# The order of the two late parts, and the last layer of expert 1 by columns, in a recurrent-attention-then-MoE kernel

## The chip, the cores and the metric

The kernel runs on one core of a Trainium2 chip. The metric is the device time of one execution in microseconds, as the median of several runs. One further execution is profiled; its trace has every instruction of TensorE (PE, with its weight loads as PEld), VectorE (DVE), ScalarE (ACT), GpSimd (POOL) and the queue of SyncE (SP).

## The reference, cut to what matters

```python
for t in range(S):                                   # B=4, H=8, S=768, D=48
    state = alpha[:, :, t, :, None] * state + k_t outer v_t
    y[:, :, t] = einsum('bhd,bhde->bhe', q[:, :, t], state)
x = y.transpose(0, 2, 1, 3).reshape(3072, 384)
# mixture of experts: 4 groups of 4 experts, F = 1024
g = argmax(x @ w_group);  e = argmax(x @ w_expert[g])
out[token] = g_w * e_w * (relu(x @ w1[g, e]) @ w2[g, e])
```

Every token goes to one of 16 experts, with the product of two softmax weights as its factor. Both layers of an expert have 384 x 1024 weights. Everything is float32.

## The kernel before, in words

**First part.** The recurrence runs in 24 chunks of 128 steps. The instructions of this part are put in order by a planner (class `Plan`, emitted at L1151): each operation has an engine, an assumed duration, the operations it comes after, and sometimes a `lead`; `level` is the longest way from an operation to the end, and of the operations that an engine could start within a patience of 0.4 us the one of the highest level goes next. PE's order and SP's order are written out by hand (`row="pe"`, `row="sp"`). The 24 chunks end in groups of tokens whose expert is chosen on DVE; each chunk's 128 rows are then scattered to the experts' slots in DRAM by an indirect DMA issued from POOL (`scatter` at L744, planned at L761). These 24 scatters are a row of their own, in which `rest` is the planned pause after one before the next may start: `REST` = 0.7 for chunks before `AHEAD_T` = 18 and 0.1 after that. `EARLY_T` is 12. A pause is no instruction: only the resulting order of the instructions reaches the chip. After the last scatter the rows of the fullest expert are fetched and turned into columns (`xt_ahead`).

**Second part.** `jobs` is a list of 18: jobs 0 and 1 are the early parts of experts 0 and 1 (96 tokens each, from the first 12 chunks), jobs 2 to 15 the other 14 experts (224 - 8 - 3r tokens, 8 less for the last two; job 15 has 169), job 16 the late part of expert 0 (120 tokens) and job 17 that of expert 1 (96 tokens). The loop at L1378 runs over them in order. For each, `hidden` makes the first layer with tokens as the moving columns (L281), 8 blocks of 128 features in 4 pairs, each pair ended by a ReLU copy on ACT (L297). For jobs 1 to 15 `result` makes the second layer the same way, "by columns": w2 is the stationary side and the tokens are the moving columns; for at most `FEW` = 124 tokens each product is made in two halves of 64 weight columns (`product`, L279). ACT copies the result to `yT` (L308). In the next job's `hidden`, `deliver_quarters` turns it back to rows on DVE (L1187), multiplies by the factors (L1190) and yields one POOL scatter of 128 quarter rows (96 floats) for each block of 32 tokens (L1194). `destined` works out the row numbers on DVE (L1229, L1237); its tile `dst_q` has two buffers, so the one of job j is written when the scatters of job j-2 are done.

Jobs 16 and 17 carry the mark `by_token`. Their second layers are kept until both first layers are done, and then made by `last_rows`, one after the other: here the hidden tokens are the stationary side and 256 and 128 columns of w2 move (L1359); DVE and ACT multiply by the factor in `marks` while copying out (L1366, L1364), and one POOL scatter of whole rows (384 floats) ends each (L1368). The scatters of job 15 are spread behind the ReLU copies of jobs 16 and 17 (`scattered` with `behind`, which puts a one-column POOL copy, L1204, ahead of a scatter).

A loop at L1411 over tokens beyond the fixed capacities follows; it turns as many times as there are such blocks.

Of the kernel before, what the change touches and what calls it, by code (L numbers as in the profile page):

```python
# [110 lines left out]
def gla_then_hierarchical_moe(  # L111
# [54 lines left out]
    FIXED, EARLY, CAPS = 2, (96, 96), (216, 192)  # L166
    LOW = 144
    FEW = 124
    EARLY_T, AHEAD_T = (B - 2) * NC, (B - 1) * NC
# [146 lines left out]
    jobs = [fixed_job(e, 0, n) for e, n in enumerate(EARLY)]  # L316
    jobs[0]["hT"] = cp.tile([P, FC, EARLY[0]], F32, name="early_hT")
    jobs += [dict(r=r, c0=0, n=cap(r), nb=-(-cap(r) // 32)) for r in range(NS)]
    jobs += [dict(e=e, c0=n, n=CAPS[e] - n, nb=-(-(CAPS[e] - n) // 32)) for e, n in enumerate(EARLY)]
    for job in jobs[-FIXED:]:  # L320
        job["by_token"] = True
    ahead = jobs[FIXED]
    ahead["rows"] = cp.tile([P, ahead["nb"], QW], F32, name="rows_ahead")
    ahead["xt"] = cp.tile([P, DC, 32 * ahead["nb"]], F32, name="xt_ahead")
# [56 lines left out]
    with ExitStack() as gla:  # L381
# [323 lines left out]
        def add_send(g, b, c0, c1, counted, weighed, after_scatter):  # L705
# [51 lines left out]
            for c in range(C):  # L757
                if C < 3:
                    plan.add(f"touch{t0 + c}", POOL, 0.1, partial(touch, t0 + c),
                             after=[f"kept_r{t0 + c}"])  # L760
                plan.add(f"scatter{t0 + c}", POOL, 1.1, partial(scatter, c),  # L761
                         after=[f"touch{t0 + c}" if C < 3 else None, placed, weighed, "rowids", f"fill{FILLS - 1}", *after_scatter],
                         row="scatter", lands=2.0, lead=LEAD if t0 + c < EARLY_T else 0.0,
                         rest=REST if t0 + c < AHEAD_T else 0.1)
                if t0 + c in BETWEEN:
                    us, fn = BETWEEN[t0 + c]
                    plan.add(f"between{t0 + c}", POOL, us, fn, row="scatter")
# [390 lines left out]
    def hidden(w1, xt, n, between={}, behind={}):  # L1158
        hT = mp.tile([P, FC, CAP], F32, name="hT")
        for f0 in range(0, FC, 2):  # L1160
            for fn in between.get(f0, ()):
                fn()
            relu(hidden_pair(w1, xt, n, f0), n, hT, f0)
            for fn in behind.get(f0, ()):
                fn(behind=hT[:, f0])
        return hT
# [172 lines left out]
    def deliver_last(k=NB):  # L1339
        waiting.extend(deliver_quarters(*pending.popleft()))  # L1340
        scattered(waiting, k)
# [28 lines left out]
            in_=yo[0:n], in_offset=None, bounds_check=N - 1, oob_is_err=False)  # L1370

    cnt, rank, order, _ = numbered
    kept = []
    fetch_rows(jobs[FIXED + 1])
    pending.append((jobs[0], results[0], destined(jobs[0])))
    results.reverse()
# [1 line left out]
    for j, job in enumerate(jobs):  # L1378
        if j == 0:
            continue  # L1380
        if j + 3 < len(jobs):
            fetch_rows(jobs[j + 3])
        width = job["n"]
        w1, w2 = weights.pop(j)
        whole = "by_token" not in job
        dst = destined(job) if whole else None
        if whole:
            hT = hidden(w1, xt, width, {2: [deliver_last] if pending else []})
        elif pending:
            one = partial(scattered, waiting, 1)  # L1390
            hT = hidden(w1, xt, width, {2: [partial(deliver_last, 1)]}, {4: [one]})
        else:
            hT = hidden(w1, xt, width, {}, {0: [one], 4: [one], 6: [partial(scattered, waiting, NB)]})
        if j + 2 < len(jobs):
            load_weights(j + 2, expert(jobs[j + 2]))
        if not whole:
            kept.append((job, w2, hT))
        if job is jobs[-1]:
            break
        xt = ahead["xt"] if jobs[j + 1] is ahead else columns(jobs[j + 1])  # L1400
        if j == 4:
            excess, ceiling = ceilings()
            first, whose, n_more = left_over()
        if whole:
            pending.append((job, result(w2, hT, width), dst))
    for a in kept:
        last_rows(*a)

    n_left = nc.values_load(n_more[0:1, 0:1], min_val=0, max_val=NX,
                            skip_runtime_bounds_check_because="a count of at most NX")  # L1410
# [92 lines left out]
```

## Time and profile before

| | |
|---|---|
| median of 3 runs | 383.19 us (381.73 to 383.92) |
| the profiled execution | 381.04 us |
| its span, first to last instruction | 379.2 us |
| PE busy | 369.1 us |
| POOL busy | 200.8 us |
| mean granted clock of TensorE | 0.997 |

The profiled execution's own time is 1.84 us above its span, and 2.15 us below the median of the three runs. The trace is read by groups of instructions, by the chain of work that ended last (followed back from the last instruction, at each step to what released it), by timelines of one engine, and by windows that give each engine's busy time in a stretch. In a timeline a line is start, duration, engine, source line, operation, output from input with their shapes; a line with xN merges N instructions that follow one another, of which it names the first's shape; in brackets is the idle time of the engine before it and what ended it.

### The profile page before, as it was taken

Reading aid. Unit: us, or ns where it says so; the run is one execution under the profiler, and the core shown is the slowest. Engines: PE = TensorE matmul, PEld = TensorE weight load, DVE = VectorE, ACT = ScalarE, POOL = GpSimd, SP = SyncE. Lnnn points to the kernel's source line nnn. Section 1 sums busy time; section 2 is a strip of 40 time slices with the busy share of each in tenths; the row PEclk is TensorE's granted clock in tenths of the full one; section 3 lists DMA queues with packets and bytes.
Section 4 is the critical chain, followed back from the end, with each engine's and each line's share of the span. In section 5 each row is a group of like instructions: output and inputs, shape, how many; then the busy total and the mean of one; then the engine's idle time right before and its main releaser. Section 6 shows DMA issues by size and latency. Waiting matters only on the chain.

```text
span 379.2 us, 10153 instructions
## 1 busy us (share of the span) xinstructions
PE 369.1 (97%) x4120; PEld 350.5 (92%) x4120; DVE 157.5 (42%) x346; ACT 119.5 (32%) x315; POOL 200.8 (53%) x241
## 2 busy tenths in 40 slices
PE   7899999999999999999999999999999999999994
PEld 5788888888879999999999999999999999999983
DVE  7799899998866420238202022020220211201200
ACT  2666757866653220211112121121211212111210
POOL 6898779999876042616254261634525326236251
PEclk9999999999999999999999999999999999999998
DMA  7999997879873599999976475866769667755001
GB/s 276 397 401 399 409 402 265 267 252 338 329 240 149 165 295 346 344 352 361 339 247 217 183 244 227 285 225 209 235 238 300 218 200 247 284 199 192 8 22 37
DMA packets 30787, 98.08 MB, mean 259 GB/s; under 512 B 18040, under 2 KB 19764, under 8 KB 26131
## 3 DMA queue, kind: packets, MB, share of 16 engines
q1 hardware_dynamic: 25955, 87.87, 66.6%
q0 software_dynamic: 4784, 9.55, 7.3%
q8 instruction: 33, 0.54, 0.6%
q14 instruction: 15, 0.12, 0.1%
HBM read 85.76 MB, written 12.07 MB: 258 GB/s over the span
## 4 chain that ended last, share of the span: by engine, by line
PE 93%; DVE 2%; issue 1%; DMA 1%; ACT 1%; POOL 0%; POOLq 0%; DVEq 0%
PE bank L281 63%; PE zs L503 6%; PE zo L569 6%; PE bank L592 5%; PE zo L578 3%; PE zo L532 3%; PE bank L545 3%; PE zs L281 2%; PE bank L1359 2%; DVE kd L469 1%; DVE cq L480 1%; DMA in<-in_rows_dram 1%; PE bank L781 1%; ACT yt L584 0%; POOL in L489 0%
## 5 line engine op out<-in xcount | busy, mean ns | idle before, releaser
L1194 POOL DMA_INDIRECT out_dram<-yq,dst_q x98 | 95.4, 974 | 146.0 <-DVE yq L1190 109.6
L281 PE MATMUL bank<-hT,w 128*64 128x96 f32 (+14 forms) x768 | 117.5, 318 | 0.0
L281 PEld LDWEIGHTS bank<-hT,w 128*128 128x128 f32 (+1 forms) x768 | 115.5, 183 | 0.0
L281 PE MATMUL bank<-xt_e,w 128*64 128x120 f32 (+14 forms) x816 | 113.5, 311 | 0.0
L281 PEld LDWEIGHTS bank<-xt_e,w 128*128 128x128 f32 (+1 forms) x816 | 111.6, 178 | 0.2 <-issue 0.2
L1237 DVE SCALAR_TENSOR_TENSOR dst_q<-xq,past_q 128x7 int32<-128x7 int32 (+1 forms) x13 | 2.2, 166 | 150.5 <-DMA out_dram<-yq,dst_q 150.5
L297 ACT ACTIVATE hT<-bank 128x192 f32<-128x192 f32 (+15 forms) x68 | 32.0, 471 | 97.7 <-PE bank L281 74.8
L308 ACT COPY yT<-bank 128x192 f32<-128x192 f32 (+28 forms) x30 | 11.9, 396 | 98.5 <-PE bank L281 98.5
L746 POOL DMA_INDIRECT slots_d<-xr,place x24 | 24.1, 1006 | 6.7 <-issue 3.6
L592 PE MATMUL bank<-wr,yt 112*64 112x116 f32 x384 | 25.7, 267 | 0.3 <-ACT yt L584 0.3
L592 PEld LDWEIGHTS bank<-wr,yt 112*64 112x64 f32 x384 | 20.6, 137 | 1.0 <-ACT yt L584 0.5
L1187 DVE STREAM_TRANSPOSE yq<-yT 128x672 f32<-128x672 f32 (+2 forms) x16 | 12.6, 789 | 18.3 <-ACT yT L308 18.3
L485 POOL TENSOR_TENSOR in<-in,kd 112x512 f32<-112x512 f32 (+1 forms) x15 | 16.7, 1118 | 5.9 <-DVE kd L469 5.9
L517 ACT COPY sm<-zs 128x512 f32<-128x512 f32 x27 | 15.8, 588 | 12.2 <-PE zs L503 11.1
L558 ACT ACTIVATE state<-sums,kd 112x48 f32<-112x48 f32 x64 | 17.9, 334 | 3.0 <-DVE sums L554 2.8
L469 DVE TENSOR_TENSOR_SCAN kd<-in,starts 112x516 f32<-112x516 f32 (+1 forms) x15 | 17.0, 1140 | 4.1 <-DMA in<-in_rows_dram 3.1
L489 POOL TENSOR_TENSOR in<-in,cq 112x512 f32<-112x512 f32 (+1 forms) x16 | 16.9, 1058 | 3.4 <-DVE cq L480 3.3
L503 PE MATMUL zs<-in 48*64 48x128 f32 (+1 forms) x352 | 16.2, 274 | 2.3 <-POOL in L489 2.2
L520 POOL TENSOR_SCALAR_AFFINE_SELECT sm<-sm 128x512 f32<-128x512 f32 x27 | 17.0, 641 | 1.6 <-ACT sm L517 1.5
L480 DVE TENSOR_TENSOR_SCAN cq<-in,starts 112x516 f32<-112x516 f32 (+1 forms) x16 | 17.3, 1090 | 1.1
L503 PEld LDWEIGHTS zs<-in 48*64 48x64 f32 (+1 forms) x352 | 13.5, 148 | 4.0 <-POOL in L489 3.2
L584 ACT COPY yt<-zo 112x512 f32<-112x512 f32 x24 | 14.1, 586 | 8.5 <-PE zo L578 6.6
(161 smaller groups left out, 406.0 us busy)
## 6 DMA issues: line engine op xcount, KB each, us to landing
w<-in_w_dram SPq DMA_DIRECT2D x36, 1536.0 KB
in<-in_rows_dram SPq DMA_DIRECT2D x11, 962.5 KB
w<-in_rows_dram SPq DMA_DIRECT2D x10, 962.5 KB
xq<-slots_d SPq DMA_DIRECT2D x28, 85.8 KB
slots_d<-blank SPq DMA_DIRECT2D x2, 980.0 KB
xq<-slots_d SPq DMA_DIRECT2D x24, 73.5 KB
out_dram<-yq,dst_q POOLq DMA_INDIRECT x98
in<-in_rows_dram SPq DMA_DIRECT2D x4, 256.0 KB
```

The source lines that it names most:

```text
L281: nc.tensor.matmul(z[s], lhsT=w[:, s], rhs=x, start=first, stop=last, skip_group_check=True)
L297: nc.scalar.activation(out=hT[:, f0:f0 + 2, 0:n], in_=z[:, 0:2 * n].rearrange("p (f t) -> p f t", f=2), func=AF.Relu)
L469: nc.vector.tensor_tensor_scan(out=flat(c.kd[:, p0:p1])[:, ::-1], data0=c.t[0:R, A1 * p1:A1 * p0:-1], data1=one_col.to_broadcast([R, A1 * ...
L480: nc.vector.tensor_tensor_scan(out=flat(c.cq[:, p0:p1]), data0=c.t[0:R, A1 * p0:A1 * p1], data1=starts[0:R, A1 * p0:A1 * p1], initial=1.0, ...
L489: nc.gpsimd.tensor_tensor(out=c.q[:, p0:p1], in0=c.q[:, p0:p1], in1=c.cq[:, p0:p1, 1:A1], op=ALU.mult)
L503: nc.tensor.matmul(c.zs[i][s, p, :], lhsT=c.k[r, p, s], rhs=c.q[r, p, :], start=True, stop=True)
L520: nc.gpsimd.affine_select(out=c.sm[:, i], in_=c.sm[:, i], pattern=[[0, HP], [1, P]], compare_op=ALU.is_ge, fill=0.0, base=0, channel_multi ...
L558: nc.scalar.activation(out=c.st[:, p, 0:D], in_=chunks[c.n - 1].sums[:, p], func=AF.Copy, scale=c.kd[:, p, 0:1])
L569: nc.tensor.matmul(of(c.zo, p)[o], lhsT=c.v[:, h * D:h * D + o.stop - o.start], rhs=c.sm[:, i, p, :], start=(p < 2), stop=(c.bc == 0), ski ...
L592: nc.tensor.matmul(z[s, p * W:(p + 1) * W], lhsT=c.yt[:, p, s], rhs=wr[:, p, :], start=True, stop=True)
L746: sent = nc.gpsimd.indirect_dma_start(out=slots_by[t], out_offset=bass.IndirectOffsetOnAxis(ap=m["place"][:, c:c + 1], axis=0), in_=xr[:, ...
L1194: nc.gpsimd.indirect_dma_start(out=out_by.popleft().rearrange("n (j w) -> (n j) w", j=4), out_offset=bass.IndirectOffsetOnAxis(ap=dst[:, b ...
```

## The change

The two late parts change places: job 16 becomes expert 1's (96 tokens), job 17 expert 0's (120 tokens). Only job 17 keeps `by_token`. Job 16's second layer is now made by `result`, by columns, after the first layers of both jobs; its rows are then turned and scattered by `deliver_last` (three scatters of quarter rows), and `last_rows` of job 17 follows. Job 16 gets `destined` in place of the row numbers in `last_rows`, and no `marks`. The scatters of job 15 keep their places in the loop. In the planner, the pause after the scatters of chunks 12 to 17 becomes 1.0 in place of 0.7, and after those of chunks 18 and 19 1.0 in place of 0.1.

```diff
-    jobs += [dict(e=e, c0=n, n=CAPS[e] - n, nb=-(-(CAPS[e] - n) // 32)) for e, n in enumerate(EARLY)]
-    for job in jobs[-FIXED:]:
-        job["by_token"] = True
+    jobs += [dict(e=e, c0=EARLY[e], n=CAPS[e] - EARLY[e], nb=-(-(CAPS[e] - EARLY[e]) // 32))
+             for e in (1, 0)]
+    jobs[-1]["by_token"] = True
...
-                         rest=REST if t0 + c < AHEAD_T else 0.1)
+                         rest=(REST if t0 + c < EARLY_T else 1.0) if t0 + c < AHEAD_T + 2 else 0.1)
...
-        if whole:
+        if job in jobs[-2:]:
+            one = partial(scattered, waiting, 1)
+            hT = hidden(w1, xt, width, *(({}, {0: [one], 4: [one], 6: [partial(scattered, waiting, NB)]})
+                                         if job is jobs[-1] else
+                                         ({2: [partial(deliver_last, 1)]}, {4: [one]})))
+        else:
             hT = hidden(w1, xt, width, {2: [deliver_last] if pending else []})
-        elif pending:
-            one = partial(scattered, waiting, 1)
-            hT = hidden(w1, xt, width, {2: [partial(deliver_last, 1)]}, {4: [one]})
-        else:
-            hT = hidden(w1, xt, width, {}, {0: [one], 4: [one], 6: [partial(scattered, waiting, NB)]})
...
-        if not whole:
-            kept.append((job, w2, hT))
...
-        if whole:
+        if job is jobs[-2]:
+            held_back = (w2, hT, width), dst
+        else:
             pending.append((job, result(w2, hT, width), dst))
-    for a in kept:
-        last_rows(*a)
+    products, dst = held_back
+    pending.append((jobs[-2], result(*products), dst))
+    deliver_last()
+    last_rows(job, w2, hT)
```

## Rows read from the trace of the kernel before

**Rows 1.** The page, busy time of each engine (share of the span, instructions)
```profile
PE 369.1 (97%) x4120; PEld 350.5 (92%) x4120; DVE 157.5 (42%) x346; ACT 119.5 (32%) x315; POOL 200.8 (53%) x241
```

**Rows 2.** The chain that ended last, in order of time (start us, us, what)
```profile
123.67 239.53 PE bank L281 x1728
363.20 7.13 PE bank L1359 x41
...
374.93 0.53 POOL out_dram L1368
```

**Rows 3.** Timeline of all engines, the last 40 us (start us, us, engine)
```profile
340.50 0.17 DVE L1237 SCALAR_TENSOR_TENSOR dst_q<-xq,past_q 128x6 int32<-128x6 int32 x1 [11.29 <-DMA out_dram<-yq,dst_q]
...
349.44 0.97 POOL L1194 DMA_INDIRECT out_dram<-yq,dst_q  x1 [0.30 <-issue]
...
354.10 9.10 PE L281 MATMUL bank<-xt_e,w 128*64 128x120 f32 x192
...
354.59 0.78 DVE L1187 STREAM_TRANSPOSE yq<-yT 128x576 f32<-128x576 f32 x1 [11.70 <-ACT yT L308]
...
356.08 0.47 DVE L1211 STREAM_TRANSPOSE xt_e<-xq 128x288 f32<-128x288 f32 x1
...
363.13 10.66 PE L1359 MATMUL bank<-w,hT 128*120 128x256 f32 x64
...
366.09 0.97 POOL L1194 DMA_INDIRECT out_dram<-yq,dst_q  x1 [0.31 <-issue]
...
368.62 0.37 ACT L1364 ACTIVATE yo<-bank,marks 120x128 f32<-120x128 f32 x1 [4.91 <-PE bank L1359]
369.30 1.02 POOL L1368 DMA_INDIRECT out_dram<-yo,dst_m  x1 [2.23 <-ACT yo L1364]
...
373.87 0.36 ACT L1364 ACTIVATE yo<-bank,marks 96x128 f32<-96x128 f32 x1 [4.88 <-PE bank L1359]
374.52 0.94 POOL L1368 DMA_INDIRECT out_dram<-yo,dst_m  x1 [4.19 <-ACT yo L1364]
```

**Rows 4.** Timeline of PE, job 1's last layer and what follows it
```profile
127.68 4.13 PE L281 MATMUL bank<-hT,w 128*64 128x96 f32 x96
131.74 9.03 PE L281 MATMUL bank<-xt_ahead,w 128*128 128x216 f32 x48
```

**Rows 5.** Timeline of ACT, the last copy of job 1's result
```profile
131.85 0.24 ACT L308 COPY yT<-bank 128x96 f32<-128x96 f32 x1 [0.29 <-PE bank L281]
```

**Rows 6.** Timeline of DVE, the ahead columns and job 0's turn
```profile
130.29 0.88 DVE L810 STREAM_TRANSPOSE xt_ahead<-rows_ahead 128x672 f32<-128x672 f32 x1 [5.08 <-DMA rows_ahead<-slots_d]
...
131.72 0.47 DVE L1187 STREAM_TRANSPOSE yq<-yT 128x288 f32<-128x288 f32 x1
132.23 0.46 DVE L1190 TENSOR_TENSOR yq<-yq,rows 128x288 f32<-128x288 f32 x1
```

**Rows 7.** Windows of 0.25 us, last two DMAs (core us, busy, PEclk, DMA, GB/s)
```profile
370.75:371.00 0.25, 0.25 (x2) 0.16 (x1) 0.00 (x0) 0.00 (x0) 0.00 (x0) 1.00 0.81 166
...
371.50:371.75 0.25, 0.25 (x3) 0.20 (x2) 0.00 (x0) 0.00 (x0) 0.00 (x0) 1.00 0.39 148
...
376.00:376.25 0.25, 0.00 (x0) 0.00 (x0) 0.00 (x0) 0.00 (x0) 0.00 (x0) 1.00 1.10 295
...
376.50:376.75 0.25, 0.00 (x0) 0.00 (x0) 0.00 (x0) 0.00 (x0) 0.00 (x0) 0.88 0.38 84
```

**Rows 8.** Windows of 1 us, after the scatters of job 14
```profile
351.00:352.00 1.00, 1.00 (x10) 1.00 (x9) 0.00 (x0) 0.00 (x0) 0.00 (x0) 1.00 0.04 7
```

**Rows 9.** Timeline of POOL, the scatter of the last chunk
```profile
121.88 0.98 POOL L746 DMA_INDIRECT slots_d<-xr,place  x1 [0.98 <-DVE cnt L348]
```

**Rows 10.** Windows by stage of the first part
```profile
60.00:85.00 25.00, 25.00 (x575) 21.88 (x572) 23.46 (x43) 17.23 (x51) 23.81 (x25) 1.00 0.80 272
85.00:113.60 28.60, 27.81 (x593) 23.46 (x591) 22.27 (x64) 17.42 (x52) 23.94 (x27) 1.00 0.86 304
113.60:123.70 10.10, 9.72 (x207) 9.10 (x207) 6.69 (x34) 3.29 (x12) 6.79 (x20) 1.00 0.41 155
```

More of the change, by code (lines that the diff above doesn't have):

```diff
@@ L1372, in gla_then_hierarchical_moe @@
     cnt, rank, order, _ = numbered
-    kept = []
     fetch_rows(jobs[FIXED + 1])
```

## The prediction

> **What bounds the kernel now.** I read four things in turn: the busy times, the chain that ended last, the last 40 us engine by engine, and the stages of the first part. The reader should see that PE is busy for 369.1 of 379.2 us, POOL for 200.8, and DVE and ACT for less than half [rows 1]. From 123.67 us on, the chain runs along PE without a gap: 239.53 us of L281 (both layers of jobs 1 to 15, and the first layers of jobs 16 and 17), then L1359, the two token-wise last layers, then the last scatter [rows 2]. So in the second part, a PE microsecond removed is a microsecond of the span until another engine becomes later. In the end itself [rows 3] PE starts the last layers at 363.13 and works 10.66 us, to 373.79; ACT copies until 374.23; POOL starts the last scatter at 374.52; the span ends 4.68 us after that. The granted clock is 1.00, the 2.4 GHz level, until the work is done [rows 7]. In the first part PE is also nearly full: idle 0.79 us from 85 to 113.6 and 0.38 us from 113.6 to 123.7, with POOL close behind it at 23.81 of 25 us from 60 to 85 [rows 10].
>
> **The last layer.** Two token-wise layers take 10.66 us [rows 3]; they have the same 32 matmul records each, whatever their number of tokens, since 256 and 128 weight columns move, so one is 5.33 us. The layer by columns for 96 tokens is in the trace: job 1's, same weights' shape, same halves. It starts at 127.68 and the next job's first matmul at 131.74 [rows 4]: 4.06 us. PE therefore ends 5.33 - 4.06 = 1.27 us earlier, at 372.52. (The part kept is the 120-token one. If it is the dearer half, for instance 5.42 against 5.24, which is where ACT's start at 368.62 would put the cut, the gain is 1.18.) I take 1.27 and keep 1.18 as the lower bound.
>
> **The exchanged first layers.** Jobs 16 and 17 need the same 192 records in 9.03 us (354.10 to 363.13) in either order: zero on PE. What may move is when their columns are there. Job 17's columns were turned from 356.08, in 0.47 us, after job 15's rows [rows 3]; PE will want the new job 17 earlier, since 96 tokens come first. The two first layers share the 9.03 us about as 96 to 120, so 96 tokens take some 4.0 us (job 1's equal stack took 4.06) and PE arrives at 358.1. The wider turn is at most 0.2 us longer: there by 356.8. Hidden by 1.3 us. On SP one small DMA (`marks`) and one row fetch fewer or more change queues that were last used 23 us before these jobs; nothing waits there.
>
> **Added before job 15's rows: `destined` for job 16.** It puts three small DVE instructions in the queue ahead of the turn of job 15's result. The last of them writes `dst_q`, which waits for the scatters of job 14; for job 15 this wait lasted 11.29 us, to 340.50 [rows 3]. The last of job 14's scatters is issued from 349.44 to 350.41, and the last of its bytes move before 352 [rows 3, 8]; the turn behind it starts at 354.59 anyway, when ACT's copy ends. Cost zero, covered by 2.6 us. If the cover were gone, the first to be late would be job 15's scatters and then job 17's columns, and PE only beyond a further 1.3 us.
>
> **Added after the first layers: turn, factor, three scatters.** Job 1 gives the distances: ACT's last copy ends at 132.09 [rows 5], 4.41 us after the layer's start, so `yT` is whole at 363.13 + 4.41 = 367.54. Turn and multiplication for 288 elements took from 131.72 to 132.69 [rows 6], so DVE has the rows at 368.55. POOL is free then: job 15's last scatter was over at 367.06, and the places of those scatters stay. DVE to POOL took 0.27 us (measured for ACT's copy to the last scatter as 374.23 to 374.52, 0.29); scatters follow at 0.97 + 0.31 = 1.28 us [rows 3]. So they run from 368.84 to 372.37. The last row scatter is wanted at 372.52 + 0.08 + 0.36 + 0.29 = 373.25. The three scatters are hidden with 0.88 us to spare (0.6, if the pause of 0.30 between scatters is kept). Below that reserve they cost nothing; beyond it each 0.1 us costs 0.1.
>
> **The end.** The last scatter carries 120 rows in place of 96. Its issue takes 1.02 in place of 0.94 us [rows 3]: 0.08. Its bytes took about 1.0 us (370.75 to 371.75) against about 0.75 (376.00 to 376.75) [rows 7]: up to 0.25 more, of which all counts if the end waits for the bytes, none if it waits for POOL's own way through the loop. I take 0.15 for both together, between bounds of 0.08 and 0.33.
>
> **The planned pauses.** They issue nothing and reach the chip as an order of instructions alone. Adding the planner's own numbers: the last scatter's level is 1.1 + 2.2 + 2.0 + 2.4 + 0.85 + 11 = 19.55; going back with the old pauses the scatter of chunk 18 stands at 28.15, 17 at 29.95, 15 at 33.55 and 12 at 38.95; with the new ones at 29.95, 32.05, 36.25 and 42.55. All that leads to them on PE's fixed list rises too: the key and query passes of chunk 23 stand above chunk 18's scatter and go from about 34.6 to 36.4. So most comparisons keep their sign: chunk 15's scatter stays below those passes. The closest pair that changes sign is chunk 16's scatter (31.75 to 34.15) against the cut of chunk 22 (31.9 to 33.7), but a scatter one pause after the last is outside the patience of 0.4, so an operation that is ready goes first either way. I cost the pauses at zero. The bounds: a gain of all the idle time left from 85 on, 0.79 + 0.38 = 1.17 us [rows 10]; a loss as in the second rival.
>
> **Sum.** -1.27 + 0.15 + 0 = -1.12 us: span 379.2 to 378.1, the profiled execution 381.04 to 379.9. The runs' median is 2.15 us above that execution; on its scale 383.19 becomes 382.1.
>
> **Rival 1: the pauses gain as well.** POOL works at 95% from 60 to 85 [rows 10], so that mask cuts ahead of scatters could spare PE some of its 1.17 us of gaps. Half to all of it gives -1.7 to -2.3, that is 381.5 to 380.9. For it: POOL makes the keys, the queries and most cut masks that PE works on, and has next to no slack there. Against: the levels hardly cross. Chance 0.14.
>
> **Rival 2, slower: the ahead columns come late.** If the order did keep the scatters apart, up to 6 x 0.3 + 2 x 0.9 = 3.6 us of pause would push the scatter of chunk 23. That scatter has 0.98 us of idle ahead of it [rows 9], and `xt_ahead` is ready at 131.17 when PE wants it at 131.74 [rows 4, 6]: 0.57 more. Delay beyond 1.55 us stalls PE one for one; at 3.6 that is 2.05, net +0.93, 384.1. It decides from a delay of 1.55 + 1.12 = 2.67 us. Against: scatters of the last chunks wait for DVE's places, not for POOL. A like loss would come from POOL passes of chunks 20 to 23 put behind a scatter, 1.2 us each. Chance 0.10, and 0.06 that it passes half a per cent.
>
> **Rival 3: the small scatters run one behind the other.** If the next scatter only started when the bytes of the one before had landed, one would take 369.30 to 371.75, 2.45 us [rows 3, 7]. Three from 368.84 end at 376.2 in place of 373.25: +2.9, net +1.8, 385.0. Against: scatters start 1.28 us apart with 0.30 idle in between [rows 3], which leaves no room for 2.45. Chance 0.03. This is where the Trainium skill speaks against the change: "DMA: Bandwidth & Descriptors", section "Anatomy of one DMA", gives each DMA issued from GpSimd a fixed cost of about 2.0 us beside its bytes. Read as a cost for each of three scatters in turn it would make an estimated 6 us, to 374.8 in place of 373.25, and the sum would be +0.4 in place of -1.12; the trace's 1.28 us from start to start shows that these fixed parts overlap, so that here only the last one counts.
>
> **Rival 4: nothing at all**, PE's gain lost in the end by a wait I don't see: 383.2. Chance 0.05.
>
> **Chances and range.** The forecast has 0.68. A measurement of this kernel can tell about half a per cent, 1.9 us, from no change, so the forecast's -1.1 counts as no change, and with it most of rivals 2 and 4. Faster by more: two thirds of rival 1 and a run or two of luck, 0.17. Slower by more: parts of rivals 2 and 3 and the same luck, 0.07. Same: 0.76. The range holds rival 1's best less a bit for the runs' scatter (their ends lie 1.5 below and 0.7 above the median), and rival 2's 384.1: 380.4 to 384.2.
>
> **What would show it.** In the changed trace: after the last first layer a stretch of L281 with 96 columns of about 4.06 us, then L1359 for about 5.3 us; three L1194 scatters ending at least half a microsecond before the last L1368 one, which starts about 1.25 us sooner; no idle of PE between the first layers; the first part's PE gaps within 0.3 us of 0.79 and 0.38; job 2's first matmul within 0.3 us of 131.74. Wrong would be: the last scatter waiting for POOL instead of ACT, a gap of PE ahead of job 2, or a first part longer or shorter by over half a microsecond.

## The result

The change makes the kernel slower. The changed kernel takes 384.66 us (median of 8 runs, 383.98 to 386.06), the kernel before, on the same chip in turn, 381.70 us (380.96 to 383.92): ratio 1.0071, 95% interval 1.0045 to 1.0097. The forecast was 382.1 us on the scale of 383.19 us, a ratio of 0.997; neither it nor its range holds. The profiled execution of the changed kernel took 386.06 us, its span is 384.4 us. It is the slowest of the eight, so its trace loses more (5.2 us of span) than the ratio does (2.7 us).

### The profile page after: what moved, and what is told of

It reads as the page before. It is cut to its first block, busy times and chain, and to the rows that moved or that the text cites. A ratio compares the mean times of both kernels' runs of the same rounds, so it can differ in the third digit from the quotient of the medians.

```text
span 384.4 us, 10287 instructions
## 1 busy us (share of the span) xinstructions
PE 370.6 (96%) x4184; PEld 350.8 (91%) x4184; DVE 158.7 (41%) x347; ACT 119.3 (31%) x316; POOL 202.6 (53%) x243
## 4 chain that ended last, share of the span: by engine, by line
PE 91%; issue 2%; DVE 2%; DMA 1%; POOL 1%; another core or an unknown queue 1%; POOLq 0%; ACT 0%; SPq 0%; DVEq 0%; ACTq 0%
PE bank L281 64%; PE zs L503 6%; PE zo L569 5%; PE bank L592 5%; PE zo L578 3%; PE bank L545 3%; PE zo L532 3%; PE zs L281 2%; DMA in<-in_rows_dram 1%; DVE kd L469 1%; DVE cq L480 1%; PE bank L781 0%; POOLq L1368 0%; POOL out_dram L1194 0%
## 5 line engine op out<-in xcount | busy, mean ns | idle before, releaser
L1194 POOL DMA_INDIRECT out_dram<-yq,dst_q x101 | 98.2, 972 | 150.5 <-DVE yq L1190 110.8
L281 PE MATMUL bank<-hT,w 128*64 128x96 f32 (+14 forms) x864 | 122.6, 311 | 0.9 <-issue 0.9
L281 PEld LDWEIGHTS bank<-hT,w 128*128 128x128 f32 (+1 forms) x864 | 119.8, 178 | 1.6 <-issue 1.6
L281 PE MATMUL bank<-xt_e,w 128*64 128x96 f32 (+14 forms) x816 | 113.5, 311 | 0.0
L1237 DVE SCALAR_TENSOR_TENSOR dst_q<-xq,past_q 128x7 int32<-128x7 int32 (+2 forms) x14 | 2.3, 166 | 160.0 <-DMA out_dram<-yq,dst_q 160.0
L503 PE MATMUL zs<-in 48*64 48x128 f32 (+1 forms) x352 | 16.2, 274 | 3.5 <-POOL in L489 2.6
L489 POOL TENSOR_TENSOR in<-in,cq 112x512 f32<-112x512 f32 (+1 forms) x16 | 16.9, 1060 | 4.2 <-DVE cq L480 3.1
L503 PEld LDWEIGHTS zs<-in 48*64 48x64 f32 (+1 forms) x352 | 13.5, 148 | 5.3 <-POOL in L489 3.6
L480 DVE TENSOR_TENSOR_SCAN cq<-in,starts 112x516 f32<-112x516 f32 (+1 forms) x16 | 17.3, 1090 | 1.1
```

The costliest lines, as they stand in the source:

```text
L281: nc.tensor.matmul(z[s], lhsT=w[:, s], rhs=x, start=first, stop=last, skip_group_check=True)
L480: nc.vector.tensor_tensor_scan(out=flat(c.cq[:, p0:p1]), data0=c.t[0:R, A1 * p0:A1 * p1], data1=starts[0:R, A1 * p0:A1 * p1], initial=1.0, ...
L489: nc.gpsimd.tensor_tensor(out=c.q[:, p0:p1], in0=c.q[:, p0:p1], in1=c.cq[:, p0:p1, 1:A1], op=ALU.mult)
L503: nc.tensor.matmul(c.zs[i][s, p, :], lhsT=c.k[r, p, s], rhs=c.q[r, p, :], start=True, stop=True)
L1194: nc.gpsimd.indirect_dma_start(out=out_by.popleft().rearrange("n (j w) -> (n j) w", j=4), out_offset=bass.IndirectOffsetOnAxis(ap=dst[:, b ...
```

## The profile after

The page's line for PE, and the chain that ended last (start, us, engine and line):

```profile
PE 370.6 (96%) x4184; PEld 350.8 (91%) x4184; DVE 158.7 (41%) x347; ACT 119.3 (31%) x316; POOL 202.6 (53%) x243
```

```profile
102.13 0.94 issue
...
127.29 241.91 PE bank L281 x1785
```

PE still carries the chain, but it begins job 1 at 127.29 instead of 123.67 [rows 2]: 3.62 us are lost in the first part, of which the line at 102.13 ("issue": PE waited for nothing that the profile shows) is one piece. What follows from job 1's first matmul to the end of the span takes 257.11 us instead of 255.53 (379.2 - 123.67): 1.58 us are lost behind it, where 1.12 were to be won. Both add up to the 5.2 us between the two spans, which are given to 0.1 us.

The first part by windows (us, busy time of PE, PEld, DVE, ACT, POOL, then the granted clock, DMA share and GB/s) answers to [rows 10]: PE is idle 1.73 us from 85 to 113.6, in place of 0.79.

```profile
60.00:85.00 25.00, 25.00 (x572) 21.90 (x573) 23.47 (x43) 17.43 (x52) 23.61 (x25) 1.00 0.80 270
85.00:113.60 28.60, 26.87 (x558) 22.20 (x556) 22.33 (x59) 17.00 (x50) 22.60 (x24) 1.00 0.79 279
```

The end, from the timeline of all engines, answers to [rows 3]:

```profile
355.49 0.16 DVE L1237 SCALAR_TENSOR_TENSOR dst_q<-xq,past_q 128x3 int32<-128x3 int32 x1 [8.78 <-DMA out_dram<-yq,dst_q]
357.72 9.10 PE L281 MATMUL bank<-xt_e,w 128*64 128x96 f32 x192
359.70 0.57 DVE L1211 STREAM_TRANSPOSE xt_e<-xq 128x384 f32<-128x384 f32 x1
...
366.65 3.03 PE L281 MATMUL bank<-hT,w 128*64 128x96 f32 x62
369.98 0.46 PE L281 MATMUL bank<-hT,w 128*64 128x96 f32 x5 [0.31 <-issue]
370.73 0.46 PE L281 MATMUL bank<-hT,w 128*64 128x96 f32 x5 [0.28 <-issue]
371.48 1.22 PE L281 MATMUL bank<-hT,w 128*64 128x96 f32 x24 [0.29 <-issue]
372.63 5.46 PE L1359 MATMUL bank<-w,hT 128*120 128x256 f32 x32
374.26 0.97 POOL L1194 DMA_INDIRECT out_dram<-yq,dst_q  x1 [3.51 <-DVE past_m L1347]
375.53 0.97 POOL L1194 DMA_INDIRECT out_dram<-yq,dst_q  x1 [0.30 <-issue]
376.81 0.97 POOL L1194 DMA_INDIRECT out_dram<-yq,dst_q  x1 [0.31 <-issue]
378.58 0.37 ACT L1364 ACTIVATE yo<-bank,marks 120x128 f32<-120x128 f32 x1 [5.60 <-PE bank L1359]
379.25 1.02 POOL L1368 DMA_INDIRECT out_dram<-yo,dst_m  x1 [1.47 <-ACT yo L1364]
```

The layer by columns begins at 366.65 and the token-wise one at 372.63: 5.98 us, not 4.06. Its 96 matmuls come as 62, 5, 5 and 24, with three gaps that end in "issue". In the brackets the gaps are 0.88 us together, because the end of each record is modelled; counted from start to start, the groups of 5 take 0.75 us each (369.98 to 370.73 to 371.48), where 5 matmuls of a layer of 4.06 us take 0.21. The gaps are real, not lost records: ACT's copy of the first two blocks starts at 372.08, 5.43 us behind the layer's start (3.52 in run e4, whose layer by columns has no gap). Everything else of the end happens as planned: no gap between the first layers (8.93 us), the three scatters over at 377.78, 1.47 us before the last one, which waits for ACT and not for POOL.

## The experiments

Each kernel ran in turn with the kernel before on one chip; ratios are to that. Four chips were used, and they differ: e1 to e4 ran on chip 5 (the kernel before takes 382.45 us there), e5 to e8 on chip 11 (381.62), e9 to e16 on chip 4 (379.29 and 379.35), e17 and e18 on chip 9 (379.50). Which chip the change's own runs had isn't on record. "Second part" is the span from job 1's first matmul (PE's timeline) to the end, in the one profiled execution. It repeats to 0.15 us (255.53 to 255.67 in nine traces with the old ending, of three chips at least), while the time of job 1's start moves by some us from execution to execution even with the same order, and lies lower on chips 4 and 9 (121.27 to 123.27) than elsewhere (123.67 to 129.72). So the second part is read from single traces, the first part from the medians.

| kernel | median, before's (us) | ratio (95%) | job 1 at | second part |
|---|---|---|---|---|
| before (profile of the prediction) | | | 123.67 | 255.53 |
| the change | 384.66, 381.70 | 1.0071 (1.0045 to 1.0097) | 127.29 | 257.11 |
| e1 pauses alone | 383.08, 382.45 | 1.0021 (0.9994 to 1.0047) | 126.11 | 255.59 |
| e2 late parts alone | 383.25, 382.45 | 1.0028 (1.0008 to 1.0047) | 123.85 | 257.05 |
| e3 the change again | 384.37, 382.45 | 1.0056 (1.0039 to 1.0074) | 129.72 | 257.08 |
| e4 columns at once | 382.49, 382.45 | 1.0002 (0.9986 to 1.0019) | 126.67 | 255.93 |
| e5 32 more before | 382.51, 381.62 | 1.0019 (0.9999 to 1.0039) | 124.32 | 257.28 |
| e6 wide last layer | 382.39, 381.62 | 1.0014 (0.9994 to 1.0033) | 124.28 | 256.02 |
| e7 pauses 12 to 17 | 382.57, 381.62 | 1.0019 (0.9996 to 1.0042) | 125.18 | 255.62 |
| e8 pauses 18, 19 | 382.56, 381.62 | 1.0025 (1.0003 to 1.0048) | 124.52 | 255.58 |
| e9 order of DVE, ACT | 379.50, 379.29 | 1.0004 (0.9983 to 1.0024) | 121.99 | 255.61 |
| e10 order of POOL | 379.37, 379.29 | 1.0008 (0.9988 to 1.0028) | 121.27 | 255.53 |
| e11 half wide | 378.71, 379.29 | 0.9981 (0.9960 to 1.0003) | 121.46 | 255.24 |
| e12 wide first layer | 379.92, 379.29 | 1.0012 (0.9996 to 1.0028) | 122.25 | 256.05 |
| e13 8 long products | 380.02, 379.35 | 1.0016 (0.9997 to 1.0035) | 122.38 | 255.82 |
| e14 order of POOL, ACT | 379.64, 379.35 | 1.0014 (0.9997 to 1.0031) | 121.97 | 255.63 |
| e15 order of POOL, DVE | 379.91, 379.35 | 1.0010 (0.9998 to 1.0021) | 122.14 | 255.56 |
| e16 pauses again | 380.01, 379.35 | 1.0026 (1.0011 to 1.0041) | 122.03 | 255.67 |
| e17 half wide again | 379.13, 379.50 | 0.9986 (0.9972 to 1.0001) | 121.91 | 255.29 |
| e18 3 long products | 379.25, 379.50 | 0.9988 (0.9965 to 1.0011) | 123.27 | 255.53 |

### The two halves of the change: e1, e2, e3, e4

e1 is the kernel before with the planner's line of the diff, e2 the change without that line, e3 the change once more.

> The kernel before with the changed pauses alone. Theory A (the pauses changed the order of the first part, and that is the loss): in the profile of the change job 1's first matmul came at 127.29 us in place of 123.67, so this run is slower than before by 2 to 4 us, with job 1 starting after 125. Theory B (the loss is in the last layers, and the late first part of that one profile was chance): within 0.5 us of before.

> The change with the old pauses: exchanged late parts, the last layer of expert 1 by columns after both first layers, its rows turned and scattered. Theory A: the prediction's term holds without the pauses, 0.5 to 1.3 us faster than before. Theory B: the gaps of PE within the 96-column layer (5.98 us in place of the 4.06 of job 1) and a last scatter 5.15 instead of 4.68 us ahead of the end come back, 1 to 3 us slower than before.

> The change itself, again on this chip, for a second profile of it. If the gaps of PE that wait for nothing in the profile (102.1, 109.9, 121.3, 369.7 to 371.2 us) belong to the kernel, they are at the same instructions again; if they are chance of one execution, they are elsewhere or missing, and the first part starts job 1 at about 125. Time 2.5 to 3.5 us over before either way.

Both halves lose, and the losses add up: 1.0021 and 1.0028 against 1.0056 and 1.0071 together. e1's interval still holds 1, and its 0.8 us lie between its two theories; e16, the same kernel again, sets its loss clear of noise (1.0026, 1.0011 to 1.0041). So of the 3.62 us by which job 1 was late in the change's trace, the medians bear out about 1. e1's second part is that of before, e2's is that of the change, with the same gaps at the same matmuls of the layer. So the first part's loss belongs to the pauses, the end's to the late parts. e3 has the three gaps of the layer at the same matmuls (62, 5, 5, 24) and the one at L503 again (1.21 us); its other gaps of the first part (110.93, 111.71, 124.03) don't stand at the change's instructions. e2's timeline:

```profile
363.21 3.03 PE L281 MATMUL bank<-hT,w 128*64 128x96 f32 x62
366.54 0.46 PE L281 MATMUL bank<-hT,w 128*64 128x96 f32 x5 [0.30 <-issue]
```

e4 is e2 with expert 1's last layer right behind its own first layer, ahead of job 17's:

```diff
-        if job is jobs[-2]:
-            held_back = (w2, hT, width), dst
-        else:
-            pending.append((job, result(w2, hT, width), dst))
-    products, dst = held_back
-    pending.append((jobs[-2], result(*products), dst))
-    deliver_last()
+        pending.append((job, result(w2, hT, width), dst))
```

> As e2, but job 16 is an ordinary job: its last layer by columns follows its own first layer at once, and its rows are turned and scattered beside job 17's first layer. Theory A: PE's sum is the same as in e2, so 0.8 to 1.4 us faster than before, and no worse than e2. Theory B (a run of over 250 short matmuls in a row makes PE's issue late): the gaps stay and move into job 17's first layer, slower than before by 0 to 2 us.

```profile
361.11 4.13 PE L281 MATMUL bank<-hT,w 128*64 128x96 f32 x96
365.07 5.09 PE L281 MATMUL bank<-xt_e,w 128*64 128x120 f32 x96
369.93 0.37 ACT L297 ACTIVATE hT<-bank 128x240 f32<-128x240 f32 x1 [1.81 <-PE bank L281]
370.09 5.46 PE L1359 MATMUL bank<-w,hT 128*120 128x256 f32 x32
376.37 0.97 POOL L1194 DMA_INDIRECT out_dram<-yq,dst_q  x1 [0.30 <-issue]
376.99 0.37 ACT L1364 ACTIVATE yo<-bank,marks 120x128 f32<-120x128 f32 x1 [5.74 <-PE bank L1359]
377.66 1.02 POOL L1368 DMA_INDIRECT out_dram<-yo,dst_m  x1 [0.32 <-issue]
```

Now the layer by columns takes 3.96 us without a gap, and the loss comes later: job 17's third ReLU waits 1.81 us for PE (no other ReLU of the two first layers over 1.15), though PE's records show no gap, and ACT's last copy starts 6.90 us after the token-wise layer (5.41 in before, if that is cut at 5.33 us [rows 3]). POOL's scatters, now later, end at 377.34, just as ACT's last copy does (376.99 + 0.37); the last scatter follows that copy by 0.30 us, as in before (0.29), so they cost nothing yet. So the delay isn't in the layer by columns as such: it comes in the third layer of short matmuls in a row, whichever that is. e2 and e4 ran on one chip. By the median e4 loses nothing against before (1.0002), but it doesn't win the 0.8 to 1.4 us of its theory A either.

### What stops PE: e5, e6, e11, e12, e13, e17, e18

All are e2 with one edit. "Short" are the matmuls of 64 weight columns and 96 or 120 tokens, some 0.04 to 0.05 us each. In e5 PE's useless opening products are cut differently, so that the rest of its instructions stand 32 matmuls further on:

```diff
-            for i in range(n):
-                nc.tensor.matmul(z[:, 0:2 * P], lhsT=nothing[:, 0:P], rhs=nothing, start=True, stop=True)
+            whole = n - 8 if n == WARM[0] else n
+            for i in range(whole + (40 if n == WARM[0] else 0)):
+                k = 2 * P if i < whole else 48
+                nc.tensor.matmul(z[:, 0:k], lhsT=nothing[:, 0:P], rhs=nothing[:, 0:k], start=True,
+                                 stop=True)
```

> The late parts alone (pauses as before), and TensorE runs 32 matmuls more in its opening stretch, where it waits for the first loads: of the 25 products of 256 columns there, 8 are cut into 40 of 48 columns, about the same columns in all. Nothing in the last layers changes; only the place of every later instruction in TensorE's stream moves on by 32 pairs of weight load and matmul. Theory A (TensorE is held at a fixed place of its instruction stream): the three gaps of 0.3 us that e2 shows after 62, 67 and 72 matmuls of expert 1's last layer stand 32 matmuls earlier, after about 30, 35 and 40; the layer still takes 5.98 us. Theory B (they belong to the work there: a wait on ScalarE, a bank or the scatters): they stay after 62, 67 and 72. Either way the time is that of e2 within its interval, 1.0028 of before.

```profile
360.48 3.82 PE L281 MATMUL bank<-xt_e,w 128*64 128x120 f32 x70 [0.20 <-issue]
...
367.45 0.41 PE L281 MATMUL bank<-hT,w 128*64 128x96 f32 x5 [0.31 <-issue]
368.18 0.41 PE L281 MATMUL bank<-hT,w 128*64 128x96 f32 x5 [0.32 <-issue]
368.93 1.20 PE L281 MATMUL bank<-hT,w 128*64 128x96 f32 x22 [0.34 <-issue]
```

The gaps come 22 to 32 matmuls from the layer's end, as before 24 to 34: they stay with the work, not with the place in the stream (theory B). But one more gap, of 0.20 us, appears after 121 matmuls of the first layers; so the place is not quite without effect.

e6 makes the last layer with weights 128 wide (`few` replaces `FEW` in `product`):

```diff
-    pending.append((jobs[-2], result(*products), dst))
+    pending.append((jobs[-2], result(*products, few=0), dst))
```

> The late parts alone, and expert 1's last layer by columns takes its weights 128 wide instead of 64 wide: 48 matmuls of about 0.11 us instead of 96 of 0.042 us, so 5.3 us of work instead of 4.06, and half as many instructions. Theory A (instructions reach TensorE too slowly in this long run of short matmuls): the three gaps vanish, the layer takes 5.3 to 5.5 us instead of 5.98, and the kernel ends about 0.5 us sooner than e2: 1.0015 of before. Theory B (a wait that belongs to the work there): the gaps of 1.9 us in all stay, the layer takes about 7 us, and the kernel is 1 us later than e2: 1.005 of before or more.

```profile
363.74 5.60 PE L281 MATMUL bank<-hT,w 128*128 128x96 f32 x48
369.18 5.38 PE L1359 MATMUL bank<-w,hT 128*120 128x256 f32 x32
```

No gap: the layer takes 5.44 us, longer work but less time than 5.98, and ACT's last copy is back at 5.47 us behind the token-wise layer's start (5.97 in e2). A wait for an event that comes 4.8 us after the layer's start, as e2's last gap ends, would have shown in this layer as well. e5 and e6 ran on one chip, with job 1 at 124.32 and 124.28: halving the number of matmuls of this layer takes the gaps away and shortens the second part by 1.26 us. The medians, 1.0019 and 1.0014, don't show this difference, though their intervals allow it. e12 makes job 16's first layer wide instead (`few=0` in `hidden`), e11 and e17 the second half of the last layer:

```diff
-            result_in(z, w2, hT, n, d0, k, f0, f1)
+            result_in(z, w2, hT, n, d0, k, f0, f1, FEW if f0 < 4 else few)
```

> The late parts alone, and of expert 1's last layer by columns the first half stays 64 wide (48 matmuls, 2.03 us), the second half goes 128 wide (24 matmuls, 2.69 us). Theory A (TensorE runs short after about 250 of these short matmuls in a row, counted over both first layers and this one): the run now ends after 240, the gaps vanish, the layer takes 4.7 to 4.9 us, 0.6 us less than in e6: 1.000 of before. Theory B (the gaps sit at this place of the layer, whatever stands there): 1.4 us of gaps stay after two thirds of the layer, 1.003 of before.

> The late parts alone, and expert 1's late first layer takes its weights 128 wide (48 matmuls, about 5.4 us instead of 4.03), while its last layer stays 64 wide. Theory A (it is the length of the run of short matmuls that counts): the run is now 192, as long as in before; no gaps, the last layer takes 4.06 us, and the kernel's time is that of e6, 1.0014 of before. Theory B (the gaps belong to the last layer itself): they stay there, 5.98 us, on top of 1.4 us more in the first layer: 1.006 of before.

> e11 once more, for its interval: the late parts alone with the second half of expert 1's last layer 128 wide. By the sum of the prediction with this layer at 4.85 us in place of 4.06: 0.4 us faster than before, 0.999; e11 measured 0.998. No gaps in the layer.

e12, then e11:

```profile
352.59 10.57 PE L281 MATMUL bank<-xt_e,w 128*128 128x96 f32 x144
362.98 4.13 PE L281 MATMUL bank<-hT,w 128*64 128x96 f32 x96
```

```profile
360.81 5.00 PE L281 MATMUL bank<-hT,w 128*64 128x96 f32 x72
365.65 5.39 PE L1359 MATMUL bank<-w,hT 128*120 128x256 f32 x32
```

e12's last layer is the very one that has three gaps in e2, with the same instructions, and takes 4.06 us (to 367.04). e11's takes 4.84 us. Both are as theory A has it. But here the matmuls are also longer. e13 and e18 leave every short one and put useless long products in front of the last layer (8, then 3; their result is used nowhere):

```diff
+    z = bank()
+    for _ in range(8):
+        nc.tensor.matmul(z[:, 0:2 * P], lhsT=nothing[:, 0:P], rhs=nothing, start=True, stop=True)
     pending.append((jobs[-2], result(*products), dst))
```

> The late parts alone, and between expert 0's late first layer and expert 1's last layer TensorE runs 8 useless products of 256 columns (about 0.9 us, 16 instructions, the array as busy as ever). Theory A (what TensorE is to do reaches it more slowly than short matmuls use it up, and 0.9 us of long ones lets the stock fill again): the gaps of the last layer shrink to 0.5 us or vanish, the layer takes 4.1 to 4.6 us, and with 0.9 us of useless work the kernel is no later than e2, rather sooner: 1.001 of before against 1.0028. Theory B (a long spell of a busy array brings the gaps, or this place does): the gaps stay at 1.9 us and the kernel is 0.9 us later than e2: 1.005.

> As e13, with 3 useless products of 256 columns (about 0.4 us, 6 instructions) instead of 8. If the stock that runs out fills again in proportion to the time given, 0.4 us takes away part of the 1.9 us: one or two of the three gaps stay, the layer takes 4.5 to 5.4 us. If any break in the run of short matmuls is enough, no gap stays, the layer takes 4.1 to 4.2 us and the kernel is 0.5 us sooner than e13, as before: 1.000. If the gaps don't hang on it, 5.98 us as in e2.

e13, then e18:

```profile
361.84 1.05 PE L1408 MATMUL bank<-nothing 128*128 128x256 bf16 x8
362.82 4.18 PE L281 MATMUL bank<-hT,w 128*64 128x96 f32 x96
366.93 5.46 PE L1359 MATMUL bank<-w,hT 128*120 128x256 f32 x32
```

```profile
362.91 0.50 PE L1408 MATMUL bank<-nothing 128*128 128x256 bf16 x3
363.34 4.18 PE L281 MATMUL bank<-hT,w 128*64 128x96 f32 x96
```

With 0.98 us of useless work in front, the layer takes 4.11 us and the second part is 1.23 us shorter than e2's; with 0.43 us it is 1.52 us shorter. This looks as if any break were enough. But e11, e12, e13, e17 and e18 ran on chips 4 and 9, and no kernel with three short layers in an unbroken row ran there: none of them shows that the gaps would have come without its edit. ACT's copies speak for a difference of the chips. Up to the end of the two first layers e2, e13 and e18 have the same instructions in the second part. The third and fourth ReLU copy of job 16, in e2 (chip 5), then in e13 (chip 4):

```profile
358.00 0.33 ACT L297 ACTIVATE hT<-bank 128x192 f32<-128x192 f32 x1 [1.14 <-PE bank L281]
358.51 0.33 ACT L297 ACTIVATE hT<-bank 128x192 f32<-128x192 f32 x1 [0.18 <-PE bank L281]
```

```profile
356.04 0.33 ACT L297 ACTIVATE hT<-bank 128x192 f32<-128x192 f32 x1 [0.66 <-PE bank L281]
357.03 0.33 ACT L297 ACTIVATE hT<-bank 128x192 f32<-128x192 f32 x1 [0.66 <-PE bank L281]
```

In e2 the third comes 1.47 us after the second and the fourth 0.51 us after the third (1.43 and 0.55 in e6, chip 11); in e13 both distances are 0.99 (1.00 and 0.99 in e18). e1 and e16 are one and the same kernel, and job 17's last ReLU comes 1.84 us after the one ahead on chip 5, 0.99 us on chip 4. So on chips 5 and 11 PE is late at times within the first 192 short matmuls, and in these traces of chips 4 and 9 it isn't, before any break. Whether the breaks took the gaps away, or these chips have none, stays open: the late parts without any further edit on chip 4 or 9 would tell.

### The pauses: e7, e8, e9, e10, e14, e15, e16

e7 and e8 are before with one half of the changed line each (1.0 for chunks 12 to 17; 1.0 for 18 and 19).

> The kernel before with only one half of the changed pauses: 1.0 instead of 0.7 us after the scatters of chunks 12 to 17, those of chunks 18 and 19 as before at 0.1. Theory A (raising the pauses of chunks 12 to 17 is what puts other work ahead in the first part): the same as e1, 1.002 of before, job 1 starting some 2 us later than in before (126 us instead of 123.7). Theory B (it is the pauses of chunks 18 and 19 that do it): no change, 1.000, job 1 within 0.5 us of before.

> The kernel before with only the other half of the changed pauses: 1.0 instead of 0.1 us after the scatters of chunks 18 and 19, those of chunks 12 to 17 as before at 0.7. Theory A (the pauses of chunks 12 to 17 do it): no change, 1.000. Theory B (those of 18 and 19 do it, which raise the urgency of every earlier scatter in the row by up to 1.8 us): as e1, 1.002 of before, job 1 starting about 126 us.

Each half costs about as much as both (1.0019, 1.0025), and neither theory is right: either half alone gives almost the same new order. In the kernel before, POOL makes chunk 22's decayed queries (L489) at 96.66 and scatters chunk 12 behind them, at 97.99; VectorE makes the scan L480 for these queries, then the sums of the weights and the places (L727) that the scatter needs. Before, then e1:

```profile
94.99 1.23 DVE L480 TENSOR_TENSOR_SCAN cq<-in,starts 112x516 f32<-112x516 f32 x1
96.66 1.17 POOL L489 TENSOR_TENSOR in<-in,cq 112x512 f32<-112x512 f32 x1
97.22 0.25 DVE L727 TENSOR_REDUCE place<-own 128x6 int32<-128x96 f32 x1
97.99 1.01 POOL L746 DMA_INDIRECT slots_d<-xr,place  x1 [0.16 <-issue]
```

```profile
96.87 1.23 DVE L480 TENSOR_TENSOR_SCAN cq<-in,starts 112x516 f32<-112x516 f32 x1
98.28 0.25 DVE L727 TENSOR_REDUCE place<-own 128x6 int32<-128x96 f32 x1
98.81 1.01 POOL L746 DMA_INDIRECT slots_d<-xr,place  x1 [1.83 <-DVE place L727]
99.86 1.19 POOL L489 TENSOR_TENSOR in<-in,cq 112x512 f32<-112x512 f32 x1
101.10 1.11 PE L503 MATMUL zs<-in 48*64 48x128 f32 x32 [0.31 <-POOL in L489]
```

In e1 VectorE has the sums ahead of the scan, so that the scan starts at 96.87 and the places are there 1.06 us later than in before; POOL has the scatter ahead of the queries, where it waits 1.83 us for the places. The queries come 3.2 us later, and PE waits 0.31 us for them. The changed kernel has the same pair (its scatter waits 0.97 us, until 98.53), and the chain's 0.94 us at 102.13 sits among those scores (L503). But that gap isn't the pauses' own: e4 and e18, with the old pauses, have it after the same 7 of 32 matmuls (0.85 and 0.94 us), and e1 and e16 don't. And in e16, e1's kernel on chip 4, the scatter hardly waits:

```profile
97.34 1.01 POOL L746 DMA_INDIRECT slots_d<-xr,place  x1 [0.24 <-DVE place L727]
```

It loses no less for that by its ratio, so this wait is not shown to be what costs the time. To see which engine's order carries the loss, e9, e10, e14 and e15 take the changed order on some engines and the old one on the rest:

```diff
+        of = {e: deque(n for n in (other if e in FROM_CHANGED else done)
+                       if self.ops[n]["eng"] == e) for e in self.LAG}
```

> The kernel before; of the order that the changed pauses give, VectorE and ScalarE take theirs, while GpSimd, TensorE and the loads keep the order of before. Theory A (the loss of the pauses comes from GpSimd's scatters, which now stand ahead of a chunk's decayed queries and wait there for VectorE's places): as before, 1.000, no gap of TensorE among the scores at 100 to 103 us. Theory B (it comes from VectorE's and ScalarE's order): as e1, e7 and e8, 1.002.

> The kernel before; of the order that the changed pauses give, GpSimd alone takes its own, the other engines keep the order of before. Theory A (GpSimd's scatters ahead of the decayed queries cost the time): 1.002 to 1.003, the scatter near 97 to 98 us waits for VectorE, the queries after it come 1 to 2 us later than in before (96.66 us), and TensorE's scores have a gap of 0.5 us or more. Theory B (the other engines' order): as before, 1.000.

> The kernel before; GpSimd and ScalarE take the order that the changed pauses give, VectorE and TensorE keep that of before. Theory A (the loss comes from GpSimd's scatter standing ahead of a chunk's decayed queries together with VectorE's scan standing ahead of the places that this scatter needs): VectorE's places are early, the scatter waits 0.2 us at most, no loss: 1.000 to 1.001. Theory B (GpSimd's and ScalarE's orders together): 1.002.

> The kernel before; GpSimd and VectorE take the order that the changed pauses give, ScalarE and TensorE keep that of before. Theory A (as in e14): VectorE's 1.23 us scan of the queries' decay runs ahead of the places, the scatter near 98 us waits 0.4 to 1.8 us for them, the queries behind it on GpSimd are late, TensorE has a gap among the scores: 1.002. Theory B: 1.000 to 1.001.

> The pauses alone, as e1, once more: 1.002 of before if the loss of e1, e7 and e8 is real, 1.000 if it was chance. The profile: job 1's first matmul 0.8 to 2.4 us later than in before by the span's start.

e16 settles that the loss is real: 1.0026 (1.0011 to 1.0041). It doesn't settle where it sits. With POOL's order alone (e10) the places are there in time:

```profile
96.88 1.01 POOL L746 DMA_INDIRECT slots_d<-xr,place  x1 [0.17 <-issue]
97.92 1.19 POOL L489 TENSOR_TENSOR in<-in,cq 112x512 f32<-112x512 f32 x1
```

With VectorE's as well (e15) the scatter waits 0.99 us for them, as theory A said; but e9, e10, e14 and e15 lie at 1.0004, 1.0008, 1.0014 and 1.0010 with intervals of +-0.001 to 0.002, which overlap with each other and with e16. The loss is shared by several reorderings, or it is too small to be split in this way; which of them carries it stays open. All it costs lies ahead of job 1, since the second part is as before in all of them.

## Why the prediction was wrong

**"The last layer" (-1.27) failed.** It took the duration of job 1's layer [rows 4] for a layer that stands elsewhere. The work is the same, and 4.06 us is right where the layer follows one layer of 96 short matmuls (job 1; 3.96 in e4). Behind 192 of them it takes 5.98 us in the change, e2, e3 and e5: +1.92. (In e12, e13 and e18, with something longer ahead of it and on other chips, it takes 4.06 to 4.11.) The end of the token-wise layer is late with it: ACT's last copy starts 5.95 us after its start, 5.55 in e12, e13 and e18 (5.47 in e6): +0.40. Those 5.55 are 0.14 above the 5.41 of before; this is the dearer half that the lower bound of 1.18 had in part.

**"The end" (+0.15) was too low.** From the last scatter's start to the span's end it was 4.68 us in before; it is 5.15 in the changed kernel, +0.47. Nine traces with the old ending have 4.68 to 4.78, eleven with the new one 4.90 to 5.15: between their means +0.30, inside the upper bound of 0.33 but twice what was taken. Which part of it grew stays open.

**The sum with what was measured:** -1.27 + 1.92 + 0.40 + 0.14 + 0.47 - 0.10 (first layers 8.93 us instead of 9.03) = +1.56; the second part grew by 1.58. That the pieces add up shows where the time went, not why. Put the other way, e11's layer of 4.84 us would make the forecast's -1.12 into -0.34, and e11 and e17 are 0.29 and 0.24 us below before.

**"The planned pauses" (0) failed.** The step worked out levels from chunk 12's scatter on, but set only those of chunks 15 and 16 against other work (chunk 23's passes, chunk 22's cut) and found hardly a sign changed. The scatters are one row: a longer pause behind a later one raises every scatter ahead of it, and it was chunks 11 and 12 that moved ahead of the queries of chunks 21 and 22. The price is 0.8 and 1.0 us by the ratios of e1 and e16, and 0.6 and 1.2 by what e3 and the change have left beside 1.5 us at the end. These prices rest on e16: e1's interval alone would allow none. It isn't rival 2's mechanism, which expected the ahead columns late: job 2's first matmul follows job 1's by 8.07 us as before (135.36 against 127.29). Its sentence on POOL passes of late chunks behind a scatter, at 1.2 us each, names the order that came, but no run ties the loss to it: that a term put at zero costs 0.8 to 1.0 us is shown, by which wait is not.

**What held.** "The exchanged first layers": no idle of PE; job 17's columns were turned by 360.27. "Destined": `dst_q` at 355.49, ahead of the turn at 358.21, at no cost. "Turn, factor, three scatters": hidden, over 1.47 us before the last scatter. (By its own numbers the rows were due at 367.54 + 0.97 = 368.51, not 368.55; nothing rests on it.) Rival 3 did not come: the three scatters start 1.27 and 1.28 us apart, so the fixed cost of about 2.0 us for each DMA issued from GpSimd, which the Trainium skill gives ("DMA: Bandwidth & Descriptors", section "Anatomy of one DMA"), overlaps here too.

The prediction named a first part longer by over half a microsecond as a sign of failure, and it was one. It had no sign for PE falling short of work: PE's records in before show nothing of it in its two first layers, 192 short matmuls followed by long ones. ACT's copies do, faintly: job 17's first ReLU comes 1.41 us after job 16's last (360.69 against 359.28) and the next 0.57 us later, where e16 on chip 4 has 1.05 and 0.93.

**A better version.** The late parts with the last layer half wide (e11, e17) and the old pauses come out at 0.9981 and 0.9986; weighted by their intervals, 0.9984 +- 0.0012, some 0.6 us below the kernel before, on chips 4 and 9; whether the late parts alone would do as well there wasn't run. Of the 1.12 us that were hoped for, 0.29 and 0.24 show in the second part of their traces; the rest of that 0.6 is within the interval.

## What to carry to other kernels

A duration read at one place of a trace holds for the same work with the same work ahead of it; ask what the engine was doing in the 10 us before. Where PE runs hundreds of matmuls of 0.04 us in a row, try making some of them wider: in e6 a layer with more work per matmul and half as many of them took 5.44 us in place of 5.98. Keep an edit and its control on one chip, or the chip is a rival of the edit. A planner's pause is not a local thing: it raises the urgency of the whole chain ahead of it, so the new order is to be written out and compared engine by engine before it is priced.

## What the runs showed of the hardware

PE, at a granted clock of 1.00 (the 2.4 GHz level) and without any wait that the trace names, loses 1.9 us in the third layer of 96 matmuls of 0.042 us in a row (the change, e2, e3, e5) and 0.4 us more behind it (ACT's last copy in e2). In e4, where the third layer is the one with 120 columns, ACT's last copy is 1.4 us late. The window of the gaps in the changed kernel:

```profile
369.60:371.50 1.90, 1.01 (x13) 0.57 (x12) 0.00 (x0) 0.00 (x0) 0.97 (x1) 1.00 0.08 25
```

PE is busy 1.01 of 1.90 us, and DMA carries 25 GB/s: neither the clock nor traffic holds it. Halving the number of matmuls in the third layer removes the gaps on the same chip (e6 against e5). Traces with a break in the row have none either (e12, e13, e18), but they are of chips 4 and 9, where ACT's copies are evenly spaced in the same two first layers ahead of it; PE's lateness differs from chip to chip, or from execution to execution. That the instructions reach PE too slowly is a guess that fits, not shown: no run here slowed or sped up their supply by itself, and e5's further gap after 121 matmuls, with the stream 32 matmuls further on, says that the count alone doesn't decide. The Trainium skill ("Runtime: NRT & Kernel Launch", section "Instruction fetch mechanics") says that an engine's instructions are read in blocks of 16 KiB while the block before is worked on, at a cost that is mostly hidden. The traces show these transfers as the DMA queue "q8 instruction", one packet of 0.02 MB each. None starts between 366.0 and 372.7 us in the change, between 362.7 and 369.5 in e2, or between 368.6 and 375.2 in e3, and each stretch holds the whole layer with its three gaps; in e5 one starts at 367.0, beside the first gap. So the gaps don't come with the transfer of a block. Whether an earlier block came late, no run shows.

PE's records can hide such a delay: in e4 they show no gap, and only ACT's waits (1.81 us, and a last copy 1.4 us after PE's last recorded end at 375.55) tell of it. So read a layer's time from the engine that waits for it as well.
